# Packed score and gradient matmuls with the FFN fed between attention units, in a forward-and-backward kernel of a gated mix of window attention and ReGLU

## The chip, the cores and the metric

The kernel runs on one core of a Trainium2 chip. The metric is the device time of one execution in microseconds (us). The kernel before took 1463.91 us (median of 13 runs, 1460.61 to 1465.62).

PE is TensorE's matmul, PEld its weight load, DVE VectorE, ACT ScalarE, POOL GpSimd, SP SyncE; a name with q behind it is that engine's sequencer. PSUM is the memory into which these kernels' matmuls write their results, in eight banks; an eviction copies a result out of it. The granted clock is the share of TensorE's full clock that the profile shows as granted, over a stretch or a run. Matmul ends are modelled in the profile, so where a duration of TensorE's work matters I count from start to start.

## The reference

One token matrix x (2048 x 512) goes through causal attention with a window of 256 (32 heads of 16) and through a ReGLU feed-forward network (FFN) of width 1376. A sigmoid gate mixes the two. The kernel returns the output and seven gradients.

```python
g = sigmoid((x * gate_w).sum(-1, keepdims=True))
a = attention(x, wqkv, wo)     # scores masked to 0 <= q - k < 256, softmax, 32 heads of 16
b = (relu(x @ W_gate) * (x @ W_up)) @ W_down
out = g * a + (1 - g) * b
# outputs: out, and the gradients of x, wqkv, wo, W_gate, W_up, W_down, gate_w for grad_out
```

## The kernel before

It runs in stages, one after the other: FFN forward and backward (outputs to DRAM), then attention for four chunks of eight heads, once by queries (o, dq) and once by keys (dk, dv), then the weight gradients, then a loop over 16 token blocks for out and dx. In attention, each head has its 16 rows of K and V set into a 128-row tile that is zero elsewhere, so the score matmuls contract over 128 rows of which 112 are zeros:

```python
KTz = cp.tile([P, HG, S], BF, name="KTz8")          # zero but for 16 rows of each head
psA = pa.enter_context(tc.tile_pool(name="psA", bufs=3, space=PSUM))   # ST, dPT: 3 buffers
for j in range(NT):                                  # 16 query blocks, by queries
    for h8 in range(HG):                             # 8 heads
        for i, kb in enumerate(kbs):                 # up to 3 key blocks
            nc.tensor.matmul(ST[:, i, :], lhsT=KTz[:, h8, kb * P:(kb + 1) * P], rhs=QT[:, j * P:(j + 1) * P], ...)
        nc.scalar.activation(PuT[:, :nb, :], ST[:, :nb, :], ACT.Exp, scale=scale)
        # ... select for the window on GpSimd
        for i, kb in enumerate(kbs):
            nc.tensor.matmul(dPT[:, i, :], lhsT=VTz[...], rhs=dOT[...], start=True, stop=True)
        nc.vector.tensor_tensor(out=PdPT[:, :nb, :], in0=PuT[:, :nb, :], in1=dPT[:, :nb, :], op=ALU.mult)
        for i, kb in enumerate(kbs):                 # 33 and 17 moving columns
            nc.tensor.matmul(Bacc[:, h8, :], lhsT=PuT[:, i, :], rhs=KV1[:, kb, h8, :], ...)
            nc.tensor.matmul(Aacc[:, h8, :], lhsT=PdPT[:, i, :], rhs=KV1[:, kb, h8, 0:17], ...)
    # ... (cut) row sums, o, dq; the same again by keys for dk, dv
```

The softmax here doesn't subtract the row's maximum and nothing guards it: scores larger than these inputs give would overflow.

## Time and profile before

| stage | length, us | limit |
|---|---|---|
| head | 47 | loads |
| FFN | 283 | TensorE |
| attention | 800 | TensorE 85%, VectorE 76% |
| weight gradients | 117 | a third DMA waits |
| token loop and end | about 205 | TensorE |

The prediction below shows the lines behind this table. Two more rows of matmul groups in the kernel before (line, engine, operation, output from inputs, rows*columns of the array in use, input, count | busy us, mean ns | idle before, and what ended it):

```profile
L318 PE MATMUL ST<-QT,KTz 128*128 128x128 bf16 x1440 | 194.9, 224 | 1.0 <-DMA KTz<-KTn 0.9
L337 PE MATMUL BAp<-KV,PdPT 128*128 128x17 bf16 x1440 | 115.2, 173 | 33.5 <-DVE PdPT L331 32.0
```

Both have 128*128: the whole array is taken, for 16 useful rows in the first and for 17 moving columns in the second. That is what the change goes for.

### The profile page before, as it was taken

What the parts mean: (1) busy time and instruction counts of PE and PEld (TensorE: products, weight loads), DVE (VectorE), ACT (ScalarE), POOL (GpSimd) and SP (SyncE); (2) the same over time, 40 slices, a digit from 0 to 9 for tenths busy, and PEclk for the clock granted to TensorE, in tenths of its full rate; (3) what the DMA queues carried; (4) which work ended last, traced back from release to release, by engine and by line L of the source; (5) the groups of instructions that cost most, each with busy time, mean ns of one, the idle gap of its engine ahead of it and who ended that gap; (6) DMA issues with size and microseconds to landing.
All of it is one profiled execution on the core that took longest, in us unless ns stands there. A gap on an engine that the chain in (4) does not pass through costs nothing.

```text
span 1462.5 us, 40605 instructions
## 1 busy us (share of the span) xinstructions
PE 1228.8 (84%) x16120; PEld 885.9 (61%) x16120; DVE 806.1 (55%) x1801; ACT 733.1 (50%) x1706; POOL 674.1 (46%) x1894
## 2 busy tenths in 40 slices
PE   2899999996886998888988879988889558799996
PEld 0556656563776876777857768667778223444443
DVE  0534343434777975777957779757789202333332
ACT  0733232332775975776957759667679100311111
POOL 1434252434556863558835568535588203022111
PEclk9999999998998998997989989989989779899998
DMA  9212122123001011001030010110010792455530
GB/s 248 88 65 98 65 78 82 72 73 95 3 3 31 3 32 30 3 3 31 3 59 3 2 31 3 31 31 2 7 26 4 241 330 87 160 166 152 155 109 19
DMA packets 127249, 99.58 MB, mean 68 GB/s; under 512 B 65521, under 2 KB 112178, under 8 KB 127058
## 3 DMA queue, kind: packets, MB, share of 16 engines
q1 hardware_dynamic: 82034, 56.63, 12.7%
q10 hardware_dynamic: 40160, 27.76, 6.6%
q0 software_dynamic: 4864, 12.59, 2.9%
q8 instruction: 126, 2.06, 0.6%
q14 instruction: 65, 0.53, 0.1%
HBM read 52.92 MB, written 35.82 MB: 61 GB/s over the span
## 4 chain that ended last, share of the span: by engine, by line
PE 58%; ACT 12%; DVE 8%; POOL 7%; DMA 6%; issue 5%; ACTq 2%; SPq 1%; DVEq 0%; POOLq 0%
PE wps L227 5%; PE S L390 5%; ACT Pu L393 5%; PE dP L401 4%; ACT PuT L322 3%; POOL PuT L324 3%; PE dPT L328 3%; PE CDp L407 3%; PE pp L276 3%; PE dxps L624 3%; DVE PdPT L331 3%; PE dps L234 3%; PE gps L188 3%; PE ups L191 3%; PE BAp L334 3%
## 5 line engine op out<-in xcount | busy, mean ns | idle before, releaser
L331 DVE TENSOR_TENSOR PdPT<-PuT,dPT 128x384 bf16<-128x384 bf16 (+2 forms) x512 | 248.9, 522 | 64.9 <-POOL PuT L324 28.7
L322 ACT ACTIVATE PuT<-ST 128x384 bf16<-128x384 f32 (+2 forms) x512 | 230.6, 479 | 88.2 <-PE ST L318 65.5
L404 DVE TENSOR_TENSOR PdP<-Pu,dP 128x384 bf16<-128x384 bf16 (+2 forms) x512 | 246.5, 526 | 31.4 <-POOL Pu L397 16.2
L393 ACT ACTIVATE Pu<-S 128x384 bf16<-128x384 f32 (+2 forms) x512 | 228.8, 483 | 30.8 <-PE S L390 11.1
L390 PE MATMUL S<-KTz,QT 128*128 128x128 bf16 x1440 | 178.7, 225 | 30.7 <-DVE R L371 22.3
L324 POOL TENSOR_SCALAR_AFFINE_SELECT PuT<-PuT 128x128 bf16<-128x128 bf16 x448 | 130.8, 298 | 148.1 <-ACT PuT L322 147.8
L318 PE MATMUL ST<-QT,KTz 128*128 128x128 bf16 x1440 | 194.9, 224 | 1.0 <-DMA KTz<-KTn 0.9
L394 POOL TENSOR_SCALAR_AFFINE_SELECT Pu<-Pu 128x128 bf16<-128x128 bf16 x512 | 148.5, 292 | 47.2 <-ACT Pu L393 32.8
L401 PE MATMUL dP<-VTz,dOT 128*128 128x128 bf16 x1440 | 168.2, 222 | 0.0
L328 PE MATMUL dPT<-dOT,VTz 128*128 128x128 bf16 x1440 | 166.9, 222 | 1.3 <-DMA VTz<-VTn 1.3
L334 PE MATMUL BAp<-KV,PuT 128*128 128x33 bf16 x1440 | 117.1, 180 | 34.0 <-POOL PuT L324 31.2
L337 PE MATMUL BAp<-KV,PdPT 128*128 128x17 bf16 x1440 | 115.2, 173 | 33.5 <-DVE PdPT L331 32.0
L196 POOL TENSOR_TENSOR hT<-rg,upm 128x512 bf16<-128x512 bf16 (+1 forms) x44 | 50.6, 1152 | 194.1 <-DVE upm L194 194.1
L397 POOL TENSOR_SCALAR_AFFINE_SELECT Pu<-Pu 128x128 bf16<-128x128 bf16 x448 | 130.9, 292 | 0.0
L407 PE MATMUL CDp<-R,Pu 128*128 128x32 bf16 x1440 | 124.7, 178 | 3.2 <-POOL Pu L394 1.3
L390 PEld LDWEIGHTS <-QT 128*128 128x128 bf16 x1440 | 106.1, 100 | 29.0 <-DVE R L371 23.1
L318 PEld LDWEIGHTS <-KTz 128*128 128x128 bf16 x1440 | 115.7, 100 | 4.7 <-issue 2.9
L315 PE MATMUL ST<-mbd,ident 128*128 128x128 bf16 x512 | 114.0, 225 | 4.8 <-ACT KV L75 4.8
L337 PEld LDWEIGHTS <-PdPT 128*128 128x128 bf16 x1440 | 83.5, 98 | 52.6 <-DVE PdPT L331 48.7
L410 PE MATMUL CDp<-Qn,PdP 128*128 128x16 bf16 x1440 | 112.6, 171 | 0.6
L334 PEld LDWEIGHTS <-PuT 128*128 128x128 bf16 x1440 | 72.2, 97 | 54.8 <-POOL PuT L324 51.4
L410 PEld LDWEIGHTS <-PdP 128*128 128x128 bf16 x1440 | 88.6, 98 | 23.3 <-issue 13.0
(154 smaller groups left out, 2373.8 us busy)
## 6 DMA issues: line engine op xcount, KB each, us to landing
dqT_g<-dqkv_d SPq DMA_DIRECT2D x8, 768.0 KB, 16.4
hT_d<-hT SPq DMA_DIRECT2D x10, 512.0 KB, 2.6
dgT_d<-dgT SPq DMA_DIRECT2D x10, 512.0 KB, 3.2
duT_d<-duT SPq DMA_DIRECT2D x10, 512.0 KB, 2.9
hT_g<-hT_d SPq DMA_DIRECT2D x8, 640.0 KB, 5.7
dgT_g<-dgT_d ACTq DMA_DIRECT2D x8, 640.0 KB, 5.2
duT_g<-duT_d ACTq DMA_DIRECT2D x8, 640.0 KB, 6.3
go_t<-in_grad_out_dram POOLq DMA_DIRECT2D x32, 128.0 KB, 2.4
```

Of the source, the lines that this page charges most:

```text
L318: nc.tensor.matmul(ST[:, i, :], lhsT=KTz[:, h8, kb * P:(kb + 1) * P], rhs=QT[:, j * P:(j + 1) * P], start=False, stop=True, skip_group_che ...
L322: nc.scalar.activation(PuT[:, :nb, :], ST[:, :nb, :], ACT.Exp, scale=scale)
L324: nc.gpsimd.affine_select(out=PuT[:, 0, :], in_=PuT[:, 0, :], compare_op=ALU.is_ge, fill=0.0, base=-1, pattern=[[-1, P]], channel_multipli ...
L328: nc.tensor.matmul(dPT[:, i, :], lhsT=VTz[:, h8, kb * P:(kb + 1) * P], rhs=dOT[:, j * P:(j + 1) * P], start=True, stop=True)
L331: nc.vector.tensor_tensor(out=PdPT[:, :nb, :], in0=PuT[:, :nb, :], in1=dPT[:, :nb, :], op=ALU.mult)
L334: nc.tensor.matmul(Bacc[:, h8, :], lhsT=PuT[:, i, :], rhs=KV1[:, kb, h8, :], start=False, stop=True, skip_group_check=True)
L337: nc.tensor.matmul(Aacc[:, h8, :], lhsT=PdPT[:, i, :], rhs=KV1[:, kb, h8, 0:17], start=False, stop=True, skip_group_check=True)
L390: nc.tensor.matmul(S2[:, i, :], lhsT=QT[:, qb * P:(qb + 1) * P], rhs=KTz[:, h8, kb * P:(kb + 1) * P], start=True, stop=True)
L393: nc.scalar.activation(Pu2[:, :nb, :], S2[:, :nb, :], ACT.Exp, scale=scale)
L401: nc.tensor.matmul(dP2[:, i, :], lhsT=dOT[:, qb * P:(qb + 1) * P], rhs=VTz[:, h8, kb * P:(kb + 1) * P], start=True, stop=True)
L404: nc.vector.tensor_tensor(out=PdP2[:, :nb, :], in0=Pu2[:, :nb, :], in1=dP2[:, :nb, :], op=ALU.mult)
L410: nc.tensor.matmul(Dacc[:, h8, :], lhsT=PdP2[:, i, :], rhs=Qn[:, qb, h8, :], start=False, stop=True, skip_group_check=True)
```

## The change

The intent is to give TensorE less to do in attention by using parts of the array side by side, to give the other engines fewer and longer instructions, and to run the FFN in the holes of attention instead of ahead of it. The diff rewrites most of the kernel (some 1200 changed lines); its core, with cuts:

```diff
-                            nc.tensor.matmul(ST[:, i, :], lhsT=KTz[:, h8, kb * P:(kb + 1) * P],
-                                             rhs=QT[:, j * P:(j + 1) * P], start=False, stop=True, ...)
+            for i in (2 * u.r, 2 * u.r + 1):                 # two heads: row groups 32i
+                rs = slice(32 * i, 32 * i + 32)
+                    lst.append(lambda ...: nc.tensor.matmul(
+                        bank[:, i % 2, col * P:(col + cnt) * P], lhsT=lt[rs, ls], rhs=rt[rs, rsl], ...))
+        def sweep(acc, us, weights, use_pd, fresh=True):     # column groups 32i, up to 384 moving columns
+            for p in range(0, len(us), 2):
+                for a, b0, cnt, col in us[p].segs:
+                    for i in range(4):
+                        nc.tensor.matmul(acc[32 * i:32 * i + 32, q0:q0 + cnt * P], lhsT=weights(a, i), rhs=m[...], ...)
-                    psA = pa.enter_context(tc.tile_pool(name="psA", bufs=3, space=PSUM))
+            u.S = ps.tile([P, 2, W], F32, tag="S", bufs=1, name="S")      # 2 banks
+            u.dP = ps.tile([P, 2, W], F32, tag="dP", bufs=1, name="dP")   # 2 banks
+        for idx, (kind, n, us, j, u) in enumerate(seq):      # 384 units of two heads by up to 512 columns
+            lists = second(u)                                # dP of this unit
+            if nxt is not None:
+                lists = lists + first(nxt)                   # S of the next
+            weave(lists)                                     # interleave the row groups
+            if nxt is not None:
+                after_scores(nxt)                            # exponential, select
+            product(u)
+            if pending:
+                pending.pop(0)()                             # one sweep of an earlier stage
+            if idx % 2 == 1:
+                fill((idx + 1) / len(seq))                   # FFN and projections up to this share
```

The eight PSUM banks are then: two for S, two for dP, two for the FFN and projections ("mm"), two for the sweeps ("acc"). A scheduler puts each engine's instructions in order, so the program order is only a wish. o, dq, dk and dv are now stored transposed, which spares the token loop its transposes and gives them to the weight-gradient stage.

## The prediction

> **What bounds the kernel now.** I read the page's busy table first, then cut the span into stages, then read single groups for the price of one instruction, and last one stretch of the chain of waits for the price of a hand-over.
>
> ```profile
> PE 1228.8 (84%) x16120; PEld 885.9 (61%) x16120; DVE 806.1 (55%) x1801; ACT 733.1 (50%) x1706; POOL 674.1 (46%) x1894
> ```
>
> Over the whole span TensorE is busiest, but no engine is full. The stages (start:end, length, busy time and count for each engine, granted clock, DMA share, GB/s) tell more:
>
> ```profile
> 0.00:47.00 47.00, 16.66 (x128) 8.52 (x129) 5.89 (x16) 10.49 (x17) 9.99 (x22) 0.85 0.80 205
> 47.00:330.00 283.00, 261.13 (x1992) 170.19 (x1992) 116.76 (x168) 105.09 (x168) 108.03 (x92) 0.99 0.22 78
> 341.00:1141.00 800.00, 683.91 (x12540) 578.12 (x12538) 604.51 (x1449) 567.77 (x1449) 500.83 (x1701) 0.94 0.07 17
> 1141.00:1258.00 117.00, 70.01 (x321) 31.99 (x322) 13.16 (x28) 7.26 (x11) 17.20 (x32) 0.78 0.76 243
> 1258.00:1447.00 189.00, 188.78 (x1109) 93.88 (x1109) 63.44 (x138) 41.91 (x63) 35.50 (x47) 1.00 0.41 122
> ```
>
> Head 47 us; the FFN 283 us, pure TensorE with the other three about 60% idle; attention 800 us, with TensorE at 85% and VectorE at 76%; the weight gradients 117 us, a third of it DMA waits at a cold clock; the token loop 189 us, pure TensorE. The FFN and attention stages, 283 + 800 = 1083 us, follow one another although they need different engines.
>
> The price of one attention instruction, at two widths where there are two (busy, mean ns | idle before):
>
> ```profile
> L331 DVE TENSOR_TENSOR PdPT<-PuT,dPT 128x384 bf16<-128x384 bf16 x448 | 228.0, 546 | 31.7 <-POOL PuT L324 28.7 <-PE dPT L328 0.4
> L331 DVE TENSOR_TENSOR PdPT<-PuT,dPT 128x256 bf16<-128x256 bf16 x32 | 12.1, 412 | 0.1
> L322 ACT ACTIVATE PuT<-ST 128x384 bf16<-128x384 f32 x448 | 210.8, 500 | 66.3 <-PE ST L318 47.5 <-DVE PdPT L331 14.5 <-PE BAp L334 0.7
> L322 ACT ACTIVATE PuT<-ST 128x128 bf16<-128x128 f32 x32 | 8.7, 276 | 18.0 <-PE ST L318 17.9
> L324 POOL TENSOR_SCALAR_AFFINE_SELECT PuT<-PuT 128x128 bf16<-128x128 bf16 x448 | 130.8, 298 | 148.1 <-ACT PuT L322 147.8
> L206 DVE TENSOR_TENSOR dgT<-dh_sb,upm 128x512 bf16<-128x512 bf16 x40 | 42.7, 1097 | 8.0 <-ACT dh_sb L205 6.9
> ```
>
> The product costs (546-412)/128 = 1.05 ns an element, the exponential (500-276)/256 = 0.875. The chain of waits in two attention steps (start, us, what):
>
> ```profile
> 600.30 0.55 DVE PdPT L331
> 600.85 0.05 issue
> 600.90 0.23 PE BAp L337 x3
> 601.13 0.08 PE BAp L334 x3
> 601.22 0.18 PE dPT L328 x3
> ...
> 601.97 0.50 ACT PuT L322
> 602.47 0.06 issue
> 602.53 0.30 POOL PuT L324
> 602.83 0.05 issue
> ```
>
> A hand-over costs 0.05 to 0.06 us; a matmul of 128 columns with its weight load starts every 0.06 us (0.18/3), one of 33 columns every 0.027 (0.08/3). So TensorE's instruction issue is cheap, and many small matmuls may be packed.
>
> **What the Trainium skill says.** "TensorE: Matmul & The Clock Gate", Measured speedup vs the span model: four K=32 matmuls in different row groups reached 3.07 times, three M=32 in different column groups 2.38 times. No trace here shows it: every matmul of the kernel before uses all 128 rows. "TensorEngine Tiling (Array Packing)", Key Properties: "Changing tiling mode (not just tile) drains the TensorE"; not shown here either. "VectorE: DVE Perf Modes", The perf-mode tier table: a tensor_tensor with a PSUM operand runs at one element a cycle of 0.96 GHz, 1.04 ns; the trace's 1.05 agrees. "ScalarE: Activation LUTs", What ACT_TABLE_LOAD costs: 0.833 ns an element; the trace's 0.875 is near it.
>
> **The change part by part.** It is a rewrite. (a) Scores contract over 32 rows, not over 128 rows mostly of zeros, and the four row groups are interleaved. (b) The products with K, V, R and Q are turned round: 32 weight columns, up to 384 moving columns, four column groups. (c) Units are 1024 wide (two heads by 512 columns) instead of 384, so 1024 exponentials become 384. (d) FFN and the projections of chunks 1 to 3 are fed between the attention units. (e) S and dP have one buffer each where they had three. (f) dq, dk, dv and O are stored transposed, so the last loop has no transposes; the gradient stage transposes instead.
>
> Counting the built program's instructions for the merged stage (9183 matmuls of the 10,916 in all; 16,120 before):
>
> TensorE. The chain of waits has 12 matmuls of 512 columns in 2.59 us, 0.216 each, so a column costs 0.42 ns at full clock. Scores: 737,280 columns, 307 us if one by one. The order that the build gives breaks many groups of four into two pairs; I take 2.7 at once: 114 us. Sweeps: 921,600 columns, 384 us one by one; four at once 96, and by the issue rate of 0.027 to 0.035 us for 3520 pairs about 95 to 125: 125 us. Everything else, full array: 774,336 columns, 323 us, plus 3 ns for each of 2700 matmuls and about 32 us for 128 fp32 matmuls (my estimate, four passes): 363 us. Sum 602 us. The order changes the tiling mode 1241 times; at an estimated 0.1 us a drain (the trace's 128-column matmul lasts 0.22 us against 0.06 to the next, so 0.16 could be exposed at most) 124 us. TensorE: 726 us.
>
> VectorE. Product of 1024: 546 + 640 x 1.04 = 1.21 us, x320; 768 wide 0.95 x32, 512 wide 0.68 x32: 439 us. Four tails of 512 per stage at 0.7, 32 stages: 90. FFN upm, dhs at 0.7 and dgT at 1.1, 44 each: 110. Rest 13. Sum 652 us.
>
> ScalarE. Exponential of 1024: 500 + 640 x 0.875 = 1.06 us, x320, plus 64 smaller: 386. Ln and Exp for 1/sum 38, dkv and KV copies 38, FFN evictions 122, projections 23. Sum 607 us.
>
> GpSimd. 736 selects of 256 or 512 elements; the trace has only 128 elements at 0.29, so 0.4 and 0.7 are estimates: 362. FFN and tail products at 1.15 to 1.3: 205. Sum 567 us.
>
> Four engines lie between 567 and 726 us, so how they are coupled sets the stage. Per unit, with one buffer: product 1.21, hand-over 0.05, dP's matmuls 512 columns in two row groups 0.21 plus 0.18 drain, hand-over 0.05: 1.70 us before the next product may start, plus 0.55 us of other VectorE work per unit, of which part fits in that gap. The longer loop over two units, exponential 1.06, two masks 1.1, product 1.21, dP 0.45, hand-overs 0.2, is 4.0 us, or 2.0 a unit. With TensorE's 1.9 us a unit in the way I take 2.1 to 2.2 for 320 units and 1.6 for 64: 670 to 700 + 105 = 775 to 805. The kernel before ran attention at 85% of its busiest engine with three buffers; 726/0.85 = 854 is the other way to see it. I take 810.
>
> Head: x and grad_out (4 MB at some 205 GB/s, 20 us), transposes on TensorE, gate, first projection, store and reload (4 us): 45 us.
>
> End: leftover FFN 5; store and load of dq, 2 MB, about 12; gradients 64 x (4 x 0.056 + 4 x 0.216) = 70 and 4 of evictions; weight transposes 34 groups at 0.5 = 17; first group of the loop's tiles can only load once the gradient pools are closed, 10; token loop 16 x 50 x 0.2165 = 173 against 189; end 15. Sum 306 us against 321.
>
> Sum 45 + 810 + 306 = 1161; predicted 1160 us, 21% less.
>
> **The rivals.** First, packing does not happen: row or column groups run one after another. Then TensorE has 307 + 384 + 363 = 1054 us plus drains, and the total is above 1400: same. For it: no matmul of this kind in the trace, and the order mixes modes. Against: the skill's measured cases. If drains cost 0.2 each, 124 more: about 1260. Second, the single buffers couple the engines at 2.6 us a unit: 980 us, total 1330. For it: the trace shows that even with three buffers the product waits for the select 28.7 us and the exponential for scores 47.5. Third, the order hides nearly all, and the merged stage runs at 90% of TensorE without drains, 670 us: 1020. Fourth, VectorE's FFN product slows GpSimd and itself (1.10 us for 512 elements, against 0.55 for 384 with a PSUM operand); GpSimd is now always busy, so up to 50 us more.
>
> **Range and chances.** The merged stage between 700 and 930 us, the rest within 20: 1050 to 1290. For no gain it must take 1085 us, 2.8 a unit, which only the first rival gives. Faster 0.95, same 0.03, slower 0.02.
>
> **What would show it.** Column-group matmuls of 384 columns starting 0.03 to 0.06 us apart confirm packing; 0.16 refutes it. The product row must read near 1.21 us and the exponential near 1.06. In the merged stage no engine should pass 90% busy, and idle before the product should name dP or the select. The token loop must be near 173 us. If the merged stage takes over 930 us, either TensorE is full (drains or packing wrong) or all engines are below 70% (coupling worse than I took).

## The result, and the profile after

The changed kernel took 1247.61 us (median of 8 runs, 1245.04 to 1254.21) against 1463.91 us. The ratio is 0.853, interval 0.852 to 0.855. Ratios here are the mean time of one kernel's fast runs over that of the other's of the same rounds, so not quite the ratio of the medians. That is 14.7% less time, where 21% had been forecast; 1160 us was the predicted time and 1247 lies inside the range.

The busy line of the profile after, over the whole span:

```profile
PE 1084.9 (87%) x11044; PEld 553.4 (45%) x11044; DVE 719.3 (58%) x911; ACT 636.4 (51%) x847; POOL 619.0 (50%) x1025
```

And its stages (start:end, length, busy time and count of each engine, granted clock, DMA share, GB/s):

```profile
0.00:46.00 46.00, 29.62 (x262) 18.41 (x262) 16.33 (x34) 19.62 (x30) 25.82 (x34) 0.96 0.54 162
46.00:916.00 870.00, 787.64 (x9336) 408.65 (x9334) 620.35 (x692) 565.50 (x728) 543.94 (x924) 0.99 0.19 59
916.00:984.00 68.00, 36.55 (x236) 18.99 (x237) 8.44 (x20) 9.75 (x17) 7.79 (x11) 0.81 0.87 238
984.00:1064.00 80.00, 57.87 (x432) 32.42 (x431) 23.61 (x55) 22.82 (x40) 4.84 (x9) 0.97 0.24 75
1064.00:1220.00 156.00, 155.88 (x702) 67.67 (x703) 44.07 (x99) 17.50 (x30) 32.05 (x42) 0.99 0.41 127
1220.00:1243.40 23.40, 17.32 (x79) 7.30 (x77) 6.56 (x14) 1.17 (x2) 4.58 (x6) 0.97 0.06 22
```

The second line is the merged stage: 870 us in place of 283 + 800, with TensorE busy 91% of it and no other engine above 71%. The third and fourth are the weight gradients and the weights' transposes, 148 us; for nearly half of the first of them TensorE is idle (36.55 of 68 us busy), with the DMA engines at 0.87 and a granted clock of 0.81. The token loop (fifth line) is pure TensorE, as it was.

The product and the exponential at full width:

```profile
L483 DVE TENSOR_TENSOR Pd<-Pt,dP 128x1024 bf16<-128x1024 bf16 x320 | 390.2, 1219 | 143.6 <-POOL Pt L455 55.2 <-PE dP L445 41.4 <-PE S L445 20.9
L478 ACT ACTIVATE Pt<-S 128x1024 bf16<-128x1024 f32 x320 | 328.6, 1027 | 172.2 <-PE S L445 152.1 <-PE dP L445 10.9 <-PE acc L494 6.5
```

1219 and 1027 ns are the predicted 1.21 and 1.06 us. What TensorE itself waits for in the merged stage (waiter, releaser, us in total, times, longest):

```profile
PE dP L445 <- DVE Pd L483: 43.9, 121, 1.7
PE acc L532 <- POOL pr L521: 8.6, 17, 0.8
```

Only a third of the 384 units make TensorE wait for the product, 44 us in all. A stretch of TensorE's timeline (start, us, what; starts are real, ends modelled):

```profile
400.60 0.28 PE L445 MATMUL S<-kv,Q 32*128 32x256 bf16 x2
400.81 0.84 PE L494 MATMUL acc<-Pd,kvr 128*32 128x384 bf16 x24
401.84 0.34 PE L445 MATMUL S<-kv,Q 32*128 32x384 bf16 x2 [0.19 <-ACT Pt L478]
```

32*128 is a row group, 128*32 a column group. In the first line only two score matmuls stand together, half of what four row groups hold. The next kind starts 0.21 us later; their 256 columns stream in 0.107, so 0.10 us goes to the change of tiling mode. In the second line 24 sweep matmuls of up to 384 columns lie within 0.84 us, which is possible only side by side.

Over the whole merged stage I counted all matmul starts in the trace. Matmuls of one tiling mode that start within 12 ns of each other count as one group, which takes its longest member's columns at 2.4 columns a nanosecond (full-array matmuls of 256 columns start 0.109 us apart in this trace, those of 512 0.216); what a change of mode costs is the rest between one start and the next.

| TensorE in the merged stage, us | predicted | counted |
|---|---|---|
| scores | 114 (2.7 at once) | 162 (1.75 at once, less 14 of overlap) |
| sweeps | 125 | 115 |
| full array | 363 | 383 (of which 56 beyond streaming) |
| mode changes | 1241 x 0.1 = 124 | 1241, put at 0.1 each: 124 |
| sum | 726 | 784 |

784 of 870 is 90%. The 0.1 us is what five of the six kinds of mode change show (1090 changes, medians 0.093 to 0.108). The sixth, from sweeps to scores (151 changes), has a median of 0.316 us and a shortest tenth of at most 0.106; each of its first score matmuls waits for a semaphore, so I put it at 0.1 too and leave the rest to the 86 us in which TensorE has nothing to do. That is a choice, not a measurement. After the merged stage, the chain that ended last (start, us, what):

```profile
911.84 3.47 PE mm L328 x16
916.52 10.53 DMA dqT<-DQO_d
927.06 19.28 DMA dkvT<-DKV_d
...
952.36 8.87 SPq L704
...
975.51 7.66 DMA out_dram<-st
```

The gradients wait for dq's load until 939 us, and later for a store of finished gradients, which stands on SyncE's queue behind the weight loads (L704 is one of them).

Two theories follow. **A**: TensorE's own work, mode changes included, sets the merged stage; the term that was too small is the scores', which run less than two at a time. **B**: the loop from the exponential over select and product to the next dP, with one buffer each for S and dP, sets 2.27 us a unit (870/384), and TensorE merely runs beside it.

### The profile page after: what moved, and what is told of

Same layout as the page of the kernel before. It is cut to its first block, busy times and chain, and to the rows that moved or that the text cites. A ratio compares the mean times of both kernels' runs of the same rounds, so it can differ in the third digit from the quotient of the medians.

```text
span 1243.4 us, 27471 instructions
## 1 busy us (share of the span) xinstructions
PE 1084.9 (87%) x11044; PEld 553.4 (45%) x11044; DVE 719.3 (58%) x911; ACT 636.4 (51%) x847; POOL 619.0 (50%) x1025
## 4 chain that ended last, share of the span: by engine, by line
PE 45%; DVE 16%; ACT 11%; POOL 10%; issue 7%; DMA 4%; SPq 2%; DVEq 0%; ACTq 0%; POOLq 0%
DVE Pd L483 12%; PE dxps L832 9%; PE dP L445 6%; ACT Pt L478 5%; POOL Pt L455 5%; PE mm L318 4%; PE S L445 3%; PE bps L799 3%; PE acc L494 3%; PE acc L544 2%; PE mm L280 2%; PE mm L273 2%; POOL pr L521 2%; DMA dkvT<-DKV_d 2%; PE dw L732 1%
## 5 line engine op out<-in xcount | busy, mean ns | idle before, releaser
L483 DVE TENSOR_TENSOR Pd<-Pt,dP 128x1024 bf16<-128x1024 bf16 (+2 forms) x384 | 442.6, 1153 | 173.7 <-POOL Pt L455 65.3
L478 ACT ACTIVATE Pt<-S 128x1024 bf16<-128x1024 f32 (+2 forms) x384 | 373.7, 973 | 218.9 <-PE S L445 194.3
L455 POOL TENSOR_SCALAR_AFFINE_SELECT Pt<-Pt 128x256 bf16<-128x256 bf16 (+1 forms) x736 | 345.5, 491 | 230.2 <-ACT Pt L478 228.4
L318 PE MATMUL mm<-rw,x_r 128*128 128x256 bf16 (+1 forms) x704 | 102.1, 279 | 1.3 <-ACT rw L306 1.2
L445 PE MATMUL dP<-dO,kv 32*128 32x128 bf16 (+2 forms) x704 | 73.9, 273 | 29.2 <-DVE Pd L483 26.4
L445 PE MATMUL dP<-kv,dO 32*128 32x384 bf16 (+2 forms) x704 | 75.1, 277 | 20.1 <-DVE Pd L483 17.6
L445 PE MATMUL S<-kv,Q 32*128 32x384 bf16 (+2 forms) x704 | 86.4, 277 | 5.7 <-ACT Pt L478 5.0
L445 PE MATMUL S<-Q,kv 32*128 32x128 bf16 (+2 forms) x704 | 77.4, 276 | 3.6 <-ACT Pt L478 3.1
L832 PE MATMUL dxps<-WuT_sb,duT_g 128*128 128x512 bf16 (+1 forms) x176 | 67.7, 385 | 2.9 <-DMA duT_g<-duT_d 2.9
L832 PE MATMUL dxps<-WgT_sb,dgT_g 128*128 128x512 bf16 (+1 forms) x176 | 67.7, 385 | 0.0
L732 PE MATMUL dw<-rt,x_r 128*128 128x512 bf16 x192 | 48.4, 396 | 14.7 <-ACT rt L684 11.4
```

What stands on the lines that cost most here:

```text
L318: nc.tensor.matmul(wps[:, 0:2 * fs], lhsT=x_r[:, t, c * P:(c + 1) * P], rhs=rows[t // 8][:, t % 8, 1:3, :fs], start=(t == 0), stop=(t == N ...
L445: lst.append(lambda lt=lt, ls=ls, rt=rt, rsl=rsl, i=i, rs=rs, col=col, cnt=cnt: nc.tensor.matmul(bank[:, i % 2, col * P:(col + cnt) * P], ...
L455: nc.gpsimd.affine_select(out=v.rearrange("p h (b k) -> p h b k", b=cnt), in_=v.rearrange("p h (b k) -> p h b k", b=cnt), compare_op=ALU.i ...
L478: nc.scalar.activation(u.Pt[:, :, :u.width], u.S[:, :, :u.width], ACT.Exp, scale=scale)
L483: nc.vector.tensor_tensor(out=u.Pd[:, :, :u.width], in0=u.Pt[:, :, :u.width], in1=u.dP[:, :, :u.width], op=ALU.mult)
L732: nc.tensor.matmul(banks[c][:], lhsT=x_r[:, t, c * P:(c + 1) * P], rhs=rt[:].rearrange("p a b -> p (a b)"), start=(t == 0), stop=(t == NT ...
```

## The experiments

Twelve kernels ran. Each is set against the changed kernel by its ratio to the kernel before, as the batches ran on different chips. "Merged" is from the first exponential (46 us) to the last product, in the profiled run. The clock column is the granted clock of that stage.

| run | result | time, us | ratio | merged, us | TensorE busy in it | not busy | clock |
|---|---|---|---|---|---|---|---|
| e1 as changed | right | 1250.77 | 0.855 | 873 | 792 | 81 | 0.97 |
| e2 no FFN in attention | right | 1565.69 | 1.072 | 872 | 804 | 68 | 0.62 |
| e3 bf16 row sums | right | 1225.73 | 0.837 | 842 | 760 | 82 | 0.99 |
| e4 no selects | wrong | 1216.07 | 0.830 | 838 | 776 | 62 | 0.99 |
| e5 S and dP one buffer | right | 1680.01 | 1.146 | 1305 | | | |
| e6 sweeps in group order | right | 1279.02 | 0.873 | 899 | 848 | 51 | 1.00 |
| e7 scores in group order | right | 1261.38 | 0.860 | 875 | 774 | 101 | 0.99 |
| e8 end parts | right | 1221.26 | 0.834 | 869 | | | |
| e9 scores chained in fours | right | 1268.93 | 0.868 | 895 | 764 | 131 | 0.95 |
| e10 product in two halves | right | 1246.49 | 0.852 | 870 | 801 | 69 | 0.98 |
| e11 e2 with full-array filler | right | 1479.30 | 1.013 | 783 | 709 | 74 | 1.00 |
| e12 together | right | 1182.85 | 0.808 | 841 | 746 | 95 | 0.99 |

About 1% of the matmul records, all of them full-array ones of 512 columns, is missing in the traces of e5 to e8 and e12. Leaving out as many of e1's lowers its busy time by some 12 us, so by this estimate theirs is that much too low, and "not busy" that much too high.

The granted clock differs between runs of one and the same kernel: the changed kernel's 13 runs (9 at first, 4 as e1) have means of 0.963 to 0.976 over the whole run, and by a straight line through them a clock lower by 0.01 goes with some 8 us more. Where a difference below leans on it, I say so; such corrections are estimates.

### e1: the changed kernel again

No edit.

> The changed kernel itself, on the chip and in the rounds of the experiments, so that they have something to be set against: 1244 to 1252 us, 0.853 of the kernel before. Theory A (TensorE's own work, mode switches included, fills 785 of the 870 us of the merged stage) and theory B (the loop score, exponential, mask, product over the single-buffered score banks sets the 2.27 us per unit) expect the same here.

Ratio 0.855 (0.851 to 0.859), as first measured (0.853). Its runs spread over 1.2%, so effects under about 0.5% can't be seen here.

### e3: row sums in bf16

```diff
-                v.ri = ap_.tile([P, W], F32, tag="ri", bufs=2, name="ri")
-                nc.scalar.activation(v.ri[:], v.L[:], ACT.Ln)
-                nc.scalar.activation(v.ri[:], v.ri[:], ACT.Exp, scale=-1.0)
+                v.ln = ap_.tile([P, W], F32, tag="ln", bufs=1, name="ln")
+                v.ri = ap_.tile([P, W], BF, tag="ri", bufs=2, name="ri")
+                nc.scalar.activation(v.ln[:], v.L[:], ACT.Ln)
+                nc.scalar.activation(v.ri[:], v.ln[:], ACT.Exp, scale=-1.0)
-        rsel = mc.tile([P, 4], F32, name="rsel")
+        rsel = mc.tile([P, 4], BF, name="rsel")
```

> The reciprocal row sums and their selector go to bf16, so that the 256 fp32 transposing matmuls of 4 columns (35.9 us busy by their row, some 0.25 us for a pair in the order of starts) become short bf16 ones; nothing in the loop of exponentials and products changes. Theory A: 20 to 25 us of TensorE work go, the total falls by 18 to 25 us (1222 to 1230). Theory B: they lie beside the loop, the total falls by under 5 us.

The matmul's row in e3; in e1 it was 256 records of fp32, 35.9 us busy:

```profile
L545 PE MATMUL acc<-rsel,ri 128*128 128x4 bf16 x128 | 10.7, 167 | 0.0
```

The merged stage in e1 and in e3:

```profile
46.00:919.00 873.00, 791.59 (x9306) 407.74 (x9304) 619.92 (x691) 563.64 (x725) 543.11 (x924) 0.97 0.19 58
46.00:888.00 842.00, 759.64 (x9172) 381.01 (x9170) 616.54 (x691) 563.13 (x724) 542.62 (x923) 0.99 0.19 60
```

The ratio fell from 0.855 to 0.837, 26 us, of which some 5 may be the clock (mean 0.974 against 0.968). In the merged stage TensorE's busy time fell by 32 us and the stage by 31 (28 and 28 against the first profile of the changed kernel, whose clock was 0.99 too): TensorE's time taken away came off the stage one for one, and the loop of exponentials and products was not touched. This is what A expected and B did not. It also gives the size of the predicted term for the fp32 matmuls (32 us).

### e4: no selects

```diff
             nc.scalar.activation(u.Pt[:, :, :u.width], u.S[:, :, :u.width], ACT.Exp, scale=scale)
-            mask(u)
```

> The causal and window selects on GpSimd are left out (wrong result on purpose): 736 selects, 356 us of GpSimd, on average 0.93 us out of every unit's way from exponential to product. TensorE's instructions are the same. Theory A: GpSimd is off the bound, the total falls by under 40 us, by what TensorE's waits for products shrink (they are 44 us). Theory B: each unit's loop loses 0.93 of its 2.27 us, so the merged stage falls until TensorE's 785 us stop it: at least 80 us less, 1165 or below.

36 us less (0.830), under A's limit of 40 and far from B's 80 or more; some 10 of the 36 may be the clock (mean 0.980 against 0.968). GpSimd's busy time in the stage fell from 543 to 207 us and each unit's way from exponential to product by 0.9 us, for 0.09 us of a unit. The loop is long, but it isn't what sets the unit. TensorE's wait for the product in e4 (43.5 us in e1):

```profile
PE dP L445 <- DVE Pd L482: 23.9, 87, 0.6
```

### e10: the product in two halves

```diff
-            nc.vector.tensor_tensor(out=u.Pd[:, :, :u.width], in0=u.Pt[:, :, :u.width], in1=u.dP[:, :, :u.width],
-                                    op=ALU.mult)
+            for a, b in ((0, u.width // 2), (u.width // 2, u.width)):
+                nc.vector.tensor_tensor(out=u.Pd[:, :, a:b], in0=u.Pt[:, :, a:b], in1=u.dP[:, :, a:b], op=ALU.mult)
```

> Each product is issued as two halves, columns cut in the middle so that both banks are held until the second is done: the same elements, one more instruction, by the rows of 512, 768 and 1024 elements (0.69, 0.95, 1.22 us) 0.15 us more VectorE time for a unit, 58 us in all, VectorE busy then 680 of 870 us. The result is right. Theory A: VectorE is not the bound, the total rises by under 15 us. Theory B: the loop grows by 0.15 us times 384, the total rises by 45 to 60 us. Something between, 20 to 40, would say that both set the stage in turn.

The halves' main row in e10:

```profile
L484 DVE TENSOR_TENSOR Pd<-Pt,dP 128x512 bf16<-128x512 bf16 x640 | 411.1, 682 | 138.1 <-PE dP L445 88.5 <-PE S L445 21.3 <-POOL Pt L455 19.2
```

Two halves cost 1.364 us where one product cost 1.219, and the kernel took as long as before (0.852 against 0.855; the intervals overlap). Together with e4 this refutes B as the bound: 0.15 us more in each unit's loop costs nothing, 0.9 us less gives a tenth of it.

### e6: the sweeps, column group after column group

```diff
-            k = 0
-            for p in range(0, len(us), 2):
-                for a, b0, cnt, col in us[p].segs:
-                    for i in range(4):
-                        u = us[p + i // 2]
+            for i in range(4):
+                k = 0
+                for p in range(0, len(us), 2):
+                    for a, b0, cnt, col in us[p].segs:
+                        u = us[p + i // 2]
```

> The sweeps go column group after column group, so that neighbours in the order use the same 32 columns of the array and can't run side by side; instructions, operands and results are the same. 912384 columns one at a time are 380 us at full clock, against 133 us now, so theory A: the merged stage rises by 210 to 270 us, the total to 1450 to 1520 (more if the granted clock falls). Theory B: the loop has room in TensorE's idle tenth only, some 85 us, so here too the total must rise, by 160 us or more; the run measures what the packing of column groups is worth rather than telling A from B.

The expectation of both theories was far off: 0.873, some 27 us more instead of 160 or more. The edit did not undo the packing. Starts of sweep matmuls in e6's trace (its own time, which begins 10.5 us before the span), with their columns (the program's order is 384, 128, 256, 256, 128, 384 for one column group, and then the same for the next):

```
412.011 384    412.239 256    412.349 256    412.458 128    412.480 384
412.184 128    412.245 384    412.419 128    412.474 256    412.514 384
```

The second group's first matmul (412.245) starts 6 ns after the first group's third (412.239), while three of the first group (412.349, 412.458, 412.514) come ahead of it in the program. In the built program the four groups do stand one after the other, as the edit asks. So TensorE does not keep matmuls of different groups in the program's order, and finds most of the overlap by itself. The Trainium skill, "TensorE: Matmul & The Clock Gate", The mechanism, has matmuls as "strict FIFO, no reordering"; this trace says otherwise. What was lost is depth: the sweeps took 337 - 131 = 206 us by the count of starts, against 115.

This is also a sum against A in its plain form: TensorE was busy 56 us more (nearer 70 with the missing records), and the stage grew by 26. The time in which TensorE isn't busy is no fixed tenth; it gave way from 81 to 51 us (nearer 40). The granted clock was higher, 1.00 against 0.97 in the stage, so by the line above the same clock would have made the difference some 11 us larger.

### e7: the scores, row group after row group

```diff
-            k = 0
-            while any(k < len(l) for l in lists):
-                for l in lists:
-                    if k < len(l):
-                        l[k]()
-                k += 1
+            for l in lists:
+                for m in l:
+                    m()
```

> The score matmuls go row group after row group, so that nearly all neighbours in the order use the same 32 rows; 735232 columns one at a time are 306 us against 175 us now. Theory A: the merged stage rises by 100 to 140 us, the total to 1345 to 1390 (more if the granted clock falls). If the row groups' packing had been worth nothing because the loop waits anyway (theory B), the total rises by under 60 us.

0.860 (0.857 to 0.863) against 0.855 (0.851 to 0.859): no difference that these rounds show. By the count of starts the scores ran 1.70 at once (1.75 in e1); TensorE paired them anyway, although the built program has them in the order 64, 64, 96, 96 or 0, 0, 32, 32 of row groups. As in e6, the run says nothing on the worth of packing, because the edit hardly touched it. That the partner depends on when S and dP are free, and not on the order within the list, is likely, but not shown.

### e9: the scores chained in fours

```diff
-            k = 0
+            k, last = 0, None
             while any(k < len(l) for l in lists):
                 for l in lists:
                     if k < len(l):
-                        l[k]()
+                        if last is None:
+                            l[k]()
+                        else:
+                            with tc.issue_after(last):
+                                l[k]()
+                        last = nc.cur_bb.bb.instructions[-1]
```

> The banks stay separate, but each score matmul is chained behind the one before it, dP pair, S pair, dP pair, S pair, so that TensorE's order has 286 runs of 8 score matmuls (196 before) and 1127 mode switches where the order had 1243. Unlike the joined buffer this leaves exponential and product free of each other. Theory A (TensorE's work and drains set the merged stage, and the scores' poor packing is the mis-sized term): score streaming falls from 175 us towards 115, some 110 switches of 0.1 us go, the total falls by 40 to 75 us to 1175 to 1210. Theory B (the loop from product to the next dP and its product sets a unit, TensorE only runs beside it): S waits for dP, the exponential starts later, the total stays within 10 us of 1250 or rises.

The packing came as A wanted it: the scores' streaming fell from 175 to 127 us, the mode changes from 1240 to 1124. But the kernel became slower, 0.868, some 19 us. TensorE's busy time in the stage fell by 28 us and the rest of the stage grew by 50. The stage, and TensorE's waits in it:

```profile
46.00:941.00 895.00, 763.99 (x9335) 401.40 (x9335) 613.18 (x692) 563.12 (x727) 548.04 (x924) 0.95 0.19 58
PE dP L445 <- DVE Pd L488: 57.2, 150, 1.0
PE acc L537 <- POOL pr L526: 33.9, 28, 1.9
```

In e1 these two waits were 43.5 and 8.5 us. So theory A's remedy fails. But part of the loss is the clock: 81 us of e9's stage ran at half clock, 48 of e1's. Outside these stretches e9 finished 0.445 units per us and e1 0.446. So at full clock the better packing neither gained nor lost, as waits took back what it saved, and the 22 us by which the stage grew lie in the stretches at half clock. Why there are more of them is not shown. How much of the waiting is the chain itself (S must now wait for dP) and how much the rest of the order, which the scheduler also made anew (the sweeps are cut into more pieces), is not settled either.

### e5: S and dP as one buffer

```diff
-            u.S = ps.tile([P, 2, W], F32, tag="S", bufs=1, name="S")
+            u.S = u.SD[:, 2:4, :]
-            u.dP = ps.tile([P, 2, W], F32, tag="dP", bufs=1, name="dP")
+            u.dP = u.SD[:, 0:2, :]
...
+            sd = ps.tile([P, 4, W], F32, tag="SD", bufs=1, name="SD")   # of u.dP and nxt.S
```

> The dP banks of a unit and the S banks of the next become one four-bank buffer, so that their score matmuls can only be issued together, when both the exponential and the product have released it. In the order on TensorE 305 of the 384 units then have 8 score matmuls in a row over all four row groups, where before nearly all were pairs. TensorE's other work is the same, mode switches stay near 1220. Theory A: the streaming of the scores falls from 175 us (1.75 at a time) to 95 to 115 us (the 2.7 to 3.2 at a time that the prediction had counted on), the merged stage by 40 to 80 us, the total to 1165 to 1210. Theory B: a unit's loop now holds score, then the longer of exponential and product, then score again with no overlap of the two, so it can't become shorter; the total stays or rises, 1240 to 1300.

It failed in a way that neither theory expected: 1680 us, 15% above the kernel before. VectorE's waits in e5:

```profile
DVE Pd L483 <- ACT Pt L478: 508.0, 306, 3.0
```

Since both read one tile, the product of a unit now waits for the exponential of the next, which it has no need of. Exponential and product follow one another, a unit takes 3.3 to 3.6 us all through the stage, and TensorE idles. So this run does not test the packing. It does show what a loop that really binds looks like: the unit's time stays at 3.3 to 3.4 us while the granted clock falls from 0.98 (400 to 600 us) to 0.51 (800 to 1000 us).

### e2 and e11: attention without the FFN, and with a filler

e2 lets no FFN step start before the last unit: it reads a row of x that is rewritten, unchanged, by an operation that needs the last unit's result.

```diff
-                fill((idx + 1) / len(seq))
+                fill(0.0)
...
+        for tT in (x_T, go_T):
+            for sb in range(NSB):
+                nc.vector.scalar_tensor_tensor(out=tT[0:1, 0, sb * W:(sb + 1) * W], in0=st["last"][0:1, :], scalar=0.0,
+                                               in1=tT[0:1, 0, sb * W:(sb + 1) * W], op0=ALU.mult, op1=ALU.add)
         for _ in ffn:
             pass
```

> No FFN step can start before the last attention unit is done; everything else is unchanged. Theory A: attention alone holds about 400 us of TensorE work (score 162, sweeps 113, projections and transposes 125) and about 1360 mode switches of 0.1 us, 536 us in all, so it ends after 540 to 620 us, the FFN then takes its 262 us at a full array without switches, and the total hardly moves: 1210 to 1290. Theory B: attention keeps its 2.27 us for each of 384 units, 870 us, and the FFN's 262 us come on top: 1480 to 1530. In between, at 1290 to 1350, would be a third reading: the single-buffered banks allow a unit every 1.6 to 1.8 us, less than the 2.27 seen but more than TensorE's work alone.

1566 us, and attention alone took 872 us, as if B were right. But the stage table shows another cause, so e2 doesn't tell A from B. From e2, two stretches, during the projections and after them:

```profile
46.00:200.00 154.00, 138.30 (x1558) 61.89 (x1556) 105.14 (x117) 102.24 (x133) 92.29 (x169) 0.94 0.23 67
600.00:800.00 200.00, 186.81 (x1614) 75.66 (x1614) 119.85 (x125) 99.97 (x115) 98.32 (x188) 0.52 0.07 20
```

The third column from the end is the granted clock: 0.94, then 0.52. TensorE is busy 93% of the second stretch and runs at half its clock. Of its matmuls there, 1425 are row-group or column-group ones; the 187 of the full array have columns for 6.5 us at full clock. The longest time from one matmul's start to the next is 1.27 us between 390 and 830 us. e11 tests whether it is the kind of work:

```diff
             product(u)
+            full = mm_bank()
+            for c in range(2):
+                nc.tensor.matmul(full[:], lhsT=u.Pt[:, 0, 0:P], rhs=x_T[:, c, 0:W], start=(c == 0), stop=(c == 1))
```

> The serial kernel, whose granted clock fell to 0.5 once the projections were done although TensorE was never idle for over 2 us, with two more full-array matmuls of 512 columns put behind each unit's product (their result is not read): 768 more matmuls, 164 us of TensorE work at full clock. If the granted clock follows the full-array work in a stretch, it stays at 0.9 or above, a unit takes 2.1 to 2.2 us instead of 2.3, and the total falls from 1566 to 1490 to 1530 although there is more to do. If it follows something else (time, die, TensorE's idle gaps), the clock stays at 0.5, the added work is 328 us, and the total rises to 1750 to 1880.

From e11, the same stretches:

```profile
46.00:200.00 154.00, 139.95 (x1538) 61.57 (x1536) 101.21 (x109) 90.28 (x112) 85.52 (x158) 1.00 0.18 51
600.00:800.00 200.00, 178.34 (x2151) 80.88 (x2150) 141.19 (x145) 120.57 (x140) 117.34 (x226) 1.00 0.07 21
```

With 164 us of useless matmuls added, the kernel became 86 us faster, and the clock stayed at 0.98 to 1.00; the full array's columns in the second stretch are now worth 51 us. From 400 to 600 us it did 98 units where e2 did 86. The Trainium skill, "TensorE: Matmul & The Clock Gate", What's actually happening, gives half clock as the state after an idle window of about 3.4 us. In e2's second stretch no idle time comes near that. Nor do shorter pauses tell the stretches apart: by the count of starts TensorE streamed 77% of the time from 400 to 600 us in e2 at a clock of 0.52, 74% in the changed kernel at 1.00 and about 68% in e5 at 0.98. So here it is not idleness, but work that is nearly all on parts of the array, that goes with the half clock. e5 is a second case: its full array had columns for 91 us from 400 to 600 us, and for 4.4 us from 800 to 1000 us, where the clock was 0.51 (though TensorE also paused more there, up to 2.4 us from start to start). Only this one filler was tried; how much full-array work suffices is open.

The pair also prices the merging. In e11 attention with its filler takes 783 us and the FFN after it about 320 more; merged, both take 873. So merging is worth 230 us against the best serial form that ran, and 315 in the total against e2. How much of the FFN is hidden in the strict sense stays open, as no run has attention alone at full clock without the filler's 164 us. The FFN's full-array work goes with the high clock while it lasts.

### e8: the end

dq is loaded by quarters of the tokens, and the transposes of two tokens are issued ahead of the matmuls of the two before.

```diff
-        for c in range(DC):
-            nc.sync.dma_start(dqT[:, c, :], dqo_v[0, c])
+        for sb in range(NSB):
+            for c in range(DC):
+                nc.sync.dma_start(dqT[:, c, sb * W:(sb + 1) * W], dqo_v[0, c][:, :, sb * W:(sb + 1) * W])
...
-                    rt = t5.tile([P, 4, P], BF, tag="rt", bufs=4)
-                    tr8(rt[:], [srcT[:, c0 + k, tsl] for k in range(4)])
+                    rt = rts.pop((rnd, t))
+                    if t % 2 == 0:
+                        make_rt(8 * rnd + t // 2 + 1)      # two tokens, eight transposes, one bank
```

> Only the part after the merged stage changes: dq is loaded by quarters of the tokens, so that the first gradient product needs 0.5 MB and not 2 MB; and the transposes of the next two tokens are issued ahead of the matmuls of the present two, into one bank, so that their eviction runs beside matmuls. If the load's 23 us (predicted 12) and the gradient stage's 96 us (predicted 74) are what made the end longer than predicted, the wait falls to 8 to 14 us and the stage to 72 to 82 us: 20 to 35 us less, total 1212 to 1228. If the gradient stage is held by the DMAs that load its other operands and the weights, the total falls by under 10 us.

0.834, 31 us less. From the last FFN matmul to the first gradient matmul it now takes 9 us (24 in the changed kernel by the same count), and the gradient stage 86 us instead of 96. A pair of tokens fell from 2.84 to 2.17 us, which would make 70 us of 32 pairs; most of the rest is one stall. The chain in e8:

```profile
935.70 9.98 DMA dkvT<-DKV_d
945.69 6.64 SPq L704
...
974.30 7.34 DMA out_dram<-st
982.30 7.62 PE dw L749 x26
```

SyncE's queue issues the weight loads (L704 and after) before the stores of the first round's gradients. The stores free the buffers that the next round's evictions need, so TensorE waits 14 us until 982.

### e12: together

e3 and e8 joined, with the gradients' stores on GpSimd's queue (one of the two store lines is shown) and three transpose banks for two:

```diff
-                            nc.sync.dma_start(out_2[rows, lo:lo + 256], st5[:, w * 256:(w + 1) * 256])
+                            nc.gpsimd.dma_start(out_2[rows, lo:lo + 256], st5[:, w * 256:(w + 1) * 256])
-                pt = ps5.tile([P, 8, P], BF, tag="tr", bufs=2)
+                pt = ps5.tile([P, 8, P], BF, tag="tr", bufs=3)
-                banks = [ps5.tile([P, D], F32, tag="dw", bufs=6, name="dw") for _ in range(DC)]
+                banks = [ps5.tile([P, D], F32, tag="dw", bufs=5, name="dw") for _ in range(DC)]
```

> The two edits that helped, put together (bf16 row sums, 25 us; loads by quarters and pipelined transposes, 29 us), and two more in the part after the merged stage: the stores of the first gradients leave on GpSimd's queue instead of SyncE's, where they stood behind the weight loads for 14 us while the next round waited for their buffers; and three banks for transposes instead of two (five for gradients instead of six), which takes up to 0.45 us from each of some 16 groups of weight transposes. If the parts don't interfere: 1250 less 25, 29, 14 and 5, so 1170 to 1190, and 0.80 to 0.815 of the kernel before. If the end's edits only move the wait to the next load, 1190 to 1200. The result must be right.

1182.85 us (1178.87 to 1185.32), right, ratio 0.808 (0.807 to 0.810): as forecast, and 5% less than the changed kernel; its mean clock was higher too (0.983 against 0.968 in e1), which by the line above is worth some 12 us. Its stretch from the end of the merged stage:

```profile
887.00:980.00 93.00, 80.70 (x559) 45.45 (x567) 22.31 (x42) 23.47 (x30) 24.67 (x43) 0.93 0.65 204
```

TensorE is busy 87% of this stretch; in the changed kernel's two stretches of the same work it was 64% (94.42 of 148 us). The gradients took 77 us and the weights' transposes 12 (18 before).

## Why the prediction was right or wrong

**Right in kind and direction.** The packing happens, the FFN hides behind attention, and the drop of 216 us is where it was said to be: 283 + 800 us became 870. The first rival (no packing) and the second (2.6 us a unit) did not come. The prices were right: product 1.219 (1.21), exponential 1.027 (1.06), a mode change 0.1 (0.1, estimated), 11.00 us for a token block of the last loop (10.83). dgT was 0.73 us where 1.1 had been read off the kernel before, so the fourth rival did not come either, and VectorE had 620 us where 652 were summed.

**The size: 87 us too optimistic**, 55 of it in the merged stage (870 against 810 and the 5 for the leftover FFN, which fell into it) and 26 at the end (327 against the other 301). The head took 46 (45 predicted), and the median run is 4 us longer than the profiled span.

In the merged stage the step that failed is the scores' term, "I take 2.7 at once: 114 us". The trace shows 1.75 at once and 162 us. The order alone is not the reason: counted in the built program, it would allow 2.4 to 2.6 at once, and 3.3 to 3.8 in e9, where the trace shows 2.4. What keeps matmuls that could run together from doing so is not shown. With the full array 20 us above its term and the sweeps 10 below, TensorE had 784 us to do and not 726. In the predicted 810 us TensorE's 726 would have been 90%, and 90% is what the changed kernel shows, of the larger sum. The prediction's other way to see it, 726/0.85 = 854, was nearer the time by two errors that cancel.

But the runs show more than a mis-sized term. e9 forced the packing that the prediction had counted on, and nothing was gained at full clock, while more time at half clock made the stage 22 us longer. Packing in fours and a loop of 2.1 us a unit were summed as if both could be had; in e9, with one buffer for S and dP each, waits took back what the packing saved. Work and waiting trade places in e6 too: where the order was left alone, e3's 32 us less of TensorE's work gave 31, while e6's 56 to 70 us more cost 26. The account that fits the runs, e2 and e5 aside, is TensorE's work with its mode changes, plus some 40 to 130 us of waiting that depends on the order. Theory B by itself is refuted by e10 and e4.

At the end, the terms for dq's load and for the gradients failed. "About 12" was 23: the first gradient matmul needs all four quarters of dq's features, and their four loads landed one after the other, at 922, 927, 933 and 938 us. "70 and 4 of evictions" was 96: the transposes' evictions were exposed for each pair of tokens, 2.84 us against the 2.17 that e8 reached, and a store waited behind weight loads. e8 and e12 recover most of both. The weights' transposes (17, measured 18) were right; the first group's wait, the token loop and the tail (10 + 173 + 15 = 198) took 190.

Two slips in the prediction's text changed nothing: not every matmul of the kernel before uses 128 rows (the 96-row remainders of the FFN's width don't), and twice the drain gives 1160 + 124 = 1284, not "about 1260".

**Not in the prediction at all** was the clock. It counted on the FFN being hidden because it needs "different engines"; that merging also goes with a high granted clock, and that attention packed in this way falls to 0.5 without full-array work (e2, e11), none of its steps or rivals had.

## What to carry to other kernels

Count TensorE's time as streaming at the packing that a trace shows (the built order alone promised 2.4 to 2.6 here, and 1.75 came), plus 0.1 us for each change of tiling mode, and test with a run that removes TensorE work without touching the order; forcing better packing gained nothing here, as waits took back what it saved. Compare granted clocks before you explain a difference of a per cent or two. Where the work is mostly on row or column groups, look at the granted clock first: some full-array matmuls in between, even useless ones, may pay for themselves. In a stage that starts with large loads, put the stores on another queue than the loads, and load in the order in which the first consumer needs it.

## What the Trainium skill lacked or had wrong

- "TensorE: Matmul & The Clock Gate", What's actually happening: it ties the half clock to idle windows. e2 ran at 0.52 for hundreds of microseconds with TensorE busy 93% and no start-to-start time above 1.27 us (390 to 830 us), with nearly all its matmuls on row or column groups; with two full-array matmuls of 512 columns a unit added (e11) it ran at 1.00.
- The same page, The mechanism: it says that matmuls never start out of the program's order. In e6 a column group's first matmul started at 412.245 us, before three matmuls of another group that stand ahead of it in the program (412.349, 412.458, 412.514).
- "TensorEngine Tiling (Array Packing)", Key Properties: it says that a change of tiling mode drains TensorE, but not for how long. Here a change cost 0.093 to 0.108 us (medians of five of the six kinds of change, 1090 changes in the merged stage).
- No page has the time of GpSimd's affine selects. The changed kernel's took 0.43 us for 256 elements a partition and 0.64 for 512, on average.
